# Small tables of the opening moved between engines, and a fourth output buffer

## The chip, the cores and the metric

The kernel runs on one core of one Trainium2 chip. Times are device microseconds of one execution. The core has a matrix engine (TensorE, PE in the profile; its weight loads are PEld), VectorE (DVE), ScalarE (ACT), GpSimd (POOL) and SyncE (SP). Each runs its own queue of instructions in order, and the queues meet only at semaphores. DMAs are issued from SP, ACT or POOL.

## The reference

```python
def _attn_ref(x):                      # x: 8 x 3072 x 256
    X = np.fft.fft(x, axis=1)
    X = np.fft.fft(X, axis=2)
    return X.real.astype(np.float32)

def _moe_ref(x, mu_k, mu_r, w_k, w_v, w_r):
    x_prev = np.concatenate([np.zeros((B, 1, D)), x[:, :-1, :]], axis=1)
    xk = mu_k * x + (1.0 - mu_k) * x_prev
    xr = mu_r * x + (1.0 - mu_r) * x_prev
    k = np.maximum(xk @ w_k, 0.0)      # w_k: 256 x 1024
    v = k * k @ w_v                    # w_v: 1024 x 256
    r = 1.0 / (1.0 + np.exp(-(xr @ w_r)))
    return r * v
```

The output of the first function is the `x` of the second: the real part of a two-dimensional Fourier transform over sequence and features, then a mixing of neighbouring positions and a gated layer.

## The kernel before, in words

The transform is made of matrix products. The 3072 positions are split as 48 times 64. Because only the real part is wanted, a position is first added to its mirror image (`fold`, on DVE, from the plain rows `xp` and the mirrored rows `xm`; the mirrored rows come by indirect DMA on POOL, `load_m` and `load_m0`). Then come three products: over the 48 with the table `w_pm` (`a_sum` in batch 0, lines L582), over the features with `w_eo` (`d_units`, L604), and over the 64 with the twiddled table `m_cs` (`c_sums`, L646). Each product goes to PSUM and is evacuated to SBUF as fp16 by ACT or DVE. After that `diff` and `mix` make the mixed inputs, and chunks of 512 positions go through `k_piece` (L757), `r_item` (L784) and `v_tile` or `v_part` (L798, L810). ACT takes the rectifier and the sigmoid, DVE the squares and, in `v_out` (L820), the gate `r` times `v` into an output tile `o`, which SP writes to memory (L828). There are 48 chunks. A table of steps says what other work stands between the matrix products of the chunks, so that the transform of the next batches runs beside the layer of the present one.

Nothing of the tables is loaded; all are computed in the opening. POOL makes ramps and indices by `iota`. From them DVE makes small rows in `rw_0`, `rw_1` and `rw_turn`, the latter holding two rows, TO and SG, used for a permutation `turn`. PE multiplies pairs of rows into phases (`outer`, L334), DVE or ACT scales these to angles in whole numbers (`u_w` for `w_pm`, `ueo` for `w_eo`, `ang` for `m_cs`; `m_angles` on DVE for the first six columns, `m_angles_2` on ACT for the rest) and wraps them by a bitwise and (`wrap_angles`), and ACT takes the sine (L386 and L388, `eo_sine` L486, `m_sine` L440). The helper `ts` on L265 is DVE's tensor_scalar, so that line stands for many small operations. After the sines ACT loads the table of the sigmoid (L839) and begins to evacuate the first products (L521).

The mixing weights mu come as two rows, `mu_row`, by two DMAs from ACT's queue. `mu_rows(a)` copies them in the wanted order into `mu_p` with three copies for each half (L226, on ACT in the kernel before). PE turns `mu_p` into columns with four tiny matrix products into `mu_ps` (L843), to which two `outer` products of the rows TO and SG are added; DVE copies the six columns to `muf_t` (L851).

PE also runs matmuls with zeros (`keep_busy`, L206, the fillers), whose results nobody reads. Four of them are the first thing PE does, eight stand behind the products of the angles, and four between the mu products and the first `a_sum`.

The order of every engine's instructions is the order in which the program writes them: at the end `pin_order` ties each instruction to the one before it on its engine. So an instruction that waits holds up all that is written behind it for the same engine. In the opening the program writes, in this order: the loads and index rows; the small rows and their products; the angles; then

```python
    m_angles_2(ang_ps[1], NJ1, NJ)
    ts(w_pm[:, 0:2, WA:WA + WB], w_pm[:, 0:2, WA:WA + WB], math.sqrt(0.5), MUL)
    ts(w_pm[:, 2], w_pm[:, 0], -1.0, MUL)
    wrap_angles(NJ1, NJ)
    m_sine(0, NJ1)
    eo_sine()
    m_sine(NJ1, NJ)
```

then the first fold, the mu products, the four zero matmuls, `a_sum(0, 0, 0)`, the next fold and so on, and after `a_sum(0, 0, 4)` the function `loads()`, which on POOL makes the index rows `row_i` (L434), gathers the two halves of `wk`, patches `w_eo` (L508, L509), clears two columns of `m_cs` (L447) and loads `wv_sb` (L455).

Of the kernel before, what the change touches and what calls it, by code (L numbers as in the profile page):

```python
# [13 lines left out]
AF = mybir.ActivationFunctionType  # L14
# [6 lines left out]
def _v(ap, extra_offset, free_dims):  # L21
    new_ap = [list(ap.ap[0])] + [[s, c] for (s, c) in free_dims]
    return dataclasses.replace(ap, offset=ap.offset + extra_offset, ap=new_ap)
# [16 lines left out]
def kernel(  # L40
# [10 lines left out]
    nc = tc.nc  # L51
# [3 lines left out]
    P = 128  # L55
# [3 lines left out]
    NJ, NJ1 = 14, 6  # L59
# [4 lines left out]
    y_pool = ctx.enter_context(tc.tile_pool(name="y_sb", bufs=1))  # L64
    mix_pool = ctx.enter_context(tc.tile_pool(name="mix", bufs=1))
    k2_pool = ctx.enter_context(tc.tile_pool(name="k2", bufs=2))
    o_pool = ctx.enter_context(tc.tile_pool(name="o", bufs=3))
    psum = ctx.enter_context(tc.tile_pool(name="psum", bufs=1, space=bass.MemoryType.PSUM))


# [10 lines left out]
    def ps_v():  # L81
        return ps_slot("V", 2, 512)
# [23 lines left out]
    V = nc.vector  # L106
# [32 lines left out]
    def gather(dst, src, idx):  # L139
        nc.gpsimd.indirect_dma_start(dst, None, src, bass.IndirectOffsetOnAxis(ap=idx, axis=0))  # L140

    def load_m(b, h, o, n, idx):
        gather(xm_t[b, h][0:parts(b), XM0 + o:XM0 + o + 256 * n],
               x.rearrange("b (s r) d -> (b s) (r d)", r=n), idx)

    def load_m0(b):
        if b == 0:
            gather(xm_00[:, 1:257], x.rearrange("b s d -> (b s) d"), idx_0[:, 0:1])
        else:
            load_m(b, 0, 2048, 1, (idx_g0 if b > 1 else idx_0)[:, b:b + 1])  # L150
# [52 lines left out]
    def keep_busy(n, ps, cols=512):  # L203

        for _ in range(n):
            nc.tensor.matmul(out=ps[:, 0:cols], lhsT=zeros,  # L206
                             rhs=_v(zeros, 0, [(0, cols // P), (1, P)]), start=True, stop=True)
# [9 lines left out]
    mu_row = const.tile([2, 256], FP32)  # L217
    mu_p = const.tile([2, 2, P], FP32)
# [4 lines left out]
    def mu_rows(a):  # L223
        for p0, f0, step, n in (((0, 0, 1, 1), (1, 2, 2, 63), (64, 1, 2, 64)),
                                ((0, 128, 1, 1), (1, 254, -2, 63), (64, 255, -2, 64)))[a]:
            nc.scalar.activation(out=mu_p[:, a, p0:p0 + n], in_=_v(mu_row, f0, [(step, n)]),  # L226
                                 func=AF.Copy)

    for h in range(2):
        x_tiles(0, h)  # L230
# [19 lines left out]
    load_m(0, 1, 0, 4, idx_4[:, 1:2])  # L250
    iota(idx_0, pattern=[[S, B]], base=S, channel_multiplier=-32)
    iota(idx_0[0:1], pattern=[[S, B]], base=0, channel_multiplier=0)
    load_m0(0)

    g_all = const.tile([P, NU // 2, 256], FP16)

# [6 lines left out]
    def ts(out, in0, s1, op0, s2=None, op1=None):  # L263
        kw = {} if op1 is None else {"op1": op1}
        V.tensor_scalar(out=out, in0=in0, scalar1=s1, scalar2=s2, op0=op0, **kw)  # L265

    MUL, ADD = ALU.mult, ALU.add
# [9 lines left out]
    TO, SG = range(2)  # L277
# [5 lines left out]
    def rv(n, o, *dims, k=1):  # L283
        return _v(rw_0[0:k], P * n + o, list(dims)) if n < 6 else _v(rw_1, P * (n - 6) + o, list(dims))

    def tv(n, o, *dims):
        return _v(rw_turn, P * n + o, list(dims))

    one = ramp[0:1]
    C_0, C_1 = [(64, 2), (1, 32)], [(64, 2), (1, 32)]  # L290
# [7 lines left out]
    V.memset(rv(PH0, 64 + 47, (1, 1)), -S / 4)  # L298
    V.memset(rv(PHS0, 64 + 15, (1, 1)), S / 4)
    V.memset(rv(ONE, 0, (1, 1)), 1.0)  # L300

# [8 lines left out]
    for i in range(2):  # L312
        nc.scalar.activation(out=unit[:, i:i + 1], in_=g_i[0:2], func=AF.Copy, bias=1.0 - i,
                             scale=2.0 * i - 1.0)
    mu_rows(0)
    mu_rows(1)

    ts(rv(JR, 0, (1, P)), one, 0.0, ADD)
    ts(rv(PN, 0, (2, 64), (1, 2)), _v(one, 0, [(2, 64), (0, 2)]), 0.0, ADD)
# [49 lines left out]
    ts(ph_c, prep[:, P_C:P_C + 4], float(TURN) / S, MUL)  # L369


    V.memset(tv(SG, 0, (1, P)), 1.0)
    V.memset(tv(SG, 32, *C_1), -1.0)
    V.memset(tv(SG, 47, (64, 2)), 1.0)
    for c in range(2):
        ts(tv(TO, 32 * c, (64, 2), (1, 32)), _v(one, 32 * c, [(64, 2), (1, 32)]),
           32.0 - 64.0 * c, ADD)
    ts(tv(TO, 15, (32, 4)), _v(one, 15, [(32, 4)]), 0.0, ADD)

    ang_ps = [ps_v(), ps_v()]  # L380
    m_outer(ang_ps[0], 0, NJ1)
# [2 lines left out]
    for g in range(2):  # L384
        kw = dict(func=AF.Sin, bias=sc[:, 2 + g:3 + g], scale=sc[:, g:g + 1])
        nc.scalar.activation(out=_v(w_pm, g, [(WA + WB, 2), (2, 2), (4, NU)]),  # L386
                             in_=_v(u_w, 0, [(0, 2), (NU, 2), (1, NU)]), **kw)
        nc.scalar.activation(out=_v(w_pm, WA + g, [(WA + WB, 2), (2, NU)]),  # L388
                             in_=_v(u_w, 2 * NU, [(0, 2), (1, NU)]), **kw)

    def wrap_angles(j0, j1):
        ts(ang[:, :, j0:j1], ang[:, :, j0:j1], TURN - 1, ALU.bitwise_and)

    def m_angles_2(ps, j0, j1):
        for c in range(2):
            nc.scalar.activation(out=ang[:, c, j0:j1], in_=ps[:, 0:64 * (j1 - j0)],
                                 func=AF.Identity, bias=ph_c[:, 2 * c:2 * c + 1],
                                 scale=float(TURN) / S)

    def m_angles(ps, j0, j1, z=0):  # L400
        for c in range(2):
            for k0, k1, n in ((j0, j0 + z, 2 * c + 1), (j0 + z, j1, 2 * c))[1 - z:]:
                ts(ang[:, c, k0:k1], ps[:, 64 * (k0 - j0):64 * (k1 - j0)], float(TURN) / S, MUL,
                   ph_c[:, n:n + 1], ADD)
        if j0 == 0:
            wrap_angles(j0, j1)

    m_angles(ang_ps[0], 0, NJ1, 1)
    for c in range(2):
        ts(ueo[:, :, c], _v(prep, P_E, [(64, 2), (1, 64)]), TURN / 256.0, MUL,  # L410
           0.75 * (1 - c) * TURN, ADD)
    ts(ueo, ueo, TURN - 1, ALU.bitwise_and)
    keep_busy(NF[0], fill)

    turn = const.tile([P, P], FP16)
# [23 lines left out]
    def m_sine(j0, j1):  # L439
        nc.scalar.activation(out=m_cs[:, 0:2, j0:j1], in_=ang[:, :, j0:j1], func=AF.Sin,  # L440
                             bias=m_pi, scale=TWO_PI / TURN)
# [43 lines left out]
    def eo_sine():  # L485
        nc.scalar.activation(out=w_eo.rearrange("p a b -> p (a b)"),  # L486
                             in_=ueo.rearrange("p a c b -> p (a c b)"), func=AF.Sin,
                             bias=m_pi, scale=TWO_PI / TURN)
# [325 lines left out]
    def v_out(c, tb, n):  # L814
        b, m, i = c
        o = o_pool.tile([P, 2, 256], FP32, name="o" if n == 2 else f"o{tb}",
                        bufs=3 if n == 2 else 1)
        t0 = tb + 1 - n

        V.scalar_tensor_tensor(out=o.rearrange("p a b -> p (a b)")[:, 0:256 * n],  # L820
                               in0=st["v", t0][:, 0:256 * n], scalar=16.0,
                               in1=st["r", c][:, 256 * t0:256 * (t0 + n)],
                               op0=ALU.mult, op1=ALU.mult)
        for s in range(2):
            k = 24 * m + 8 * i + 2 * t0 + s
            dst = dataclasses.replace(out[b, k:k + 1, :], ap=[[48 * D, 64], [2 * D, n], [1, D]])
            eng = nc.scalar if s and c == chunks[-1] else nc.sync
            eng.dma_start(out=dst, in_=o[64 * s:64 * s + 64, 0:n])  # L828

    m_angles_2(ang_ps[1], NJ1, NJ)
    ts(w_pm[:, 0:2, WA:WA + WB], w_pm[:, 0:2, WA:WA + WB], math.sqrt(0.5), MUL)
    ts(w_pm[:, 2], w_pm[:, 0], -1.0, MUL)
    wrap_angles(NJ1, NJ)
    m_sine(0, NJ1)
    eo_sine()
    m_sine(NJ1, NJ)
    nc.scalar.activation(out=warm, in_=zeros[:, 0:1], func=AF.Sigmoid)  # L839
    fold(0, 0, 1, 4)  # L840
# [44 lines left out]
    for a in range(2):  # L885
        t = x_t["t", a] = mix_pool.tile([P, 24, 64], FP16, name=f"t{a}")
        nc.scalar.activation(out=t[:, 0:4],
                             in_=_v(first, 64 * a, [(128, 2), (512, 2), (1, 64)]), func=AF.Copy,
# [140 lines left out]
    for b in range(B):  # L1029
# [9 lines left out]
        if t < B:  # L1039
# [6 lines left out]
            c = [(c_pairs, t, 8 * n, (8, 8, 8, 4)[n], EV[n]) for n in range(4)]  # L1046
# [21 lines left out]
    for step in range(nk + LAG):  # L1068
        if step < nk:
            k_piece(chunks[step // 4], step % 4)  # L1070
        due(step, "x")
        v = v_steps.get(step)
        if v and step not in early_v:
            v_tile(*v)
        if step in p_steps:
            v_part(*p_steps[step])
        due(step, "e")
        if step + 1 in early_v:
            v_tile(*v_steps[step + 1])
        early = step in OUT_FIRST  # L1080
        for v in o_steps.get(step, ()) if early else ():
            v_out(*v)
        due(step, "w")
        for v in () if early else o_steps.get(step, ()):
            v_out(*v)
        if step < 4 * EARLY + 4:
            square(chunks[step // 4], step % 4, 1, step in SQUARE_A)
        elif step < nk and step % 2:
            square(chunks[step // 4], step % 4)
# [32 lines left out]
```

## Time and profile before

| | us |
|---|---|
| median of 3 runs (431.78 to 432.16) | 432.0 |
| the profiled execution | 432.3 |
| its span, first to last instruction | 430.5 |
| PE busy in it | 422.7 (98%) |
| DVE busy | 360.8 (84%) |
| ACT busy | 320.3 (74%) |
| POOL busy | 62.7 (15%) |

In the rows shown below, a row of the timeline reads: start, duration, engine, line of the kernel, operation, what it writes and reads by the program's names, shapes, and how many instructions are merged; in brackets stands how long the engine was idle before and what ended that. A row of the chain gives start, duration and what the end of the run hung on then. A row of the stretches gives the stretch, its length, the busy time of PE, PEld, DVE, ACT and POOL with their counts, the granted share of PE's clock, the share of the DMA engines and GB/s. A row of the waits gives who waited, for whom, the total, how often and the longest. Matmuls are pipelined, so the end of one lies beyond the start of the next.

### The profile page before, as it was taken

To read this page: it belongs to the slowest core of one execution; us is meant where nothing else is said; L and a number is where in the kernel's file an instruction comes from. 1 tells how busy PE (TensorE), PEld (TensorE's weight loads), DVE (VectorE), ACT (ScalarE), POOL (GpSimd) and SP (SyncE) were. 2 spreads that over 40 slices of the span, in tenths; PEclk is the share of its full clock that TensorE was granted. 3 is DMA by queue.
4 is the path that set the end of the run, shared out by engine and by line. 5 is a ranking of instruction groups with operands and counts; after the bars stand their busy time and mean duration, and the time that the engine had idled before them with its cause. 6 is when DMAs were issued, how large, how long until landed. Compare 5 with 4: busy or idle time off the path is not lost.

```text
span 430.5 us, 9306 instructions
## 1 busy us (share of the span) xinstructions
PE 422.7 (98%) x3858; PEld 298.3 (69%) x3858; DVE 360.8 (84%) x547; ACT 320.3 (74%) x373; POOL 62.7 (15%) x96
## 2 busy tenths in 40 slices
PE   7999999999999999999999999999999999999996
PEld 3666766777777776776677777777776767766765
DVE  8898989997998879988898988989799847997453
ACT  7888898867778778776877777777786867666661
POOL 7686202000050001400041000500000000000000
PEclk9999999999999999999999999999999999999999
DMA  8999926323286232933259223763232322223233
GB/s 172 143 146 197 224 58 123 81 50 73 61 144 153 59 77 56 191 95 75 52 113 188 64 50 74 136 158 75 50 75 49 75 69 55 68 64 72 67 73 99
DMA packets 35102, 42.06 MB, mean 98 GB/s; under 512 B 4114, under 2 KB 31092, under 8 KB 35060
## 3 DMA queue, kind: packets, MB, share of 16 engines
q1 hardware_dynamic: 27488, 25.41, 23.6%
q0 software_dynamic: 7264, 15.80, 22.4%
q8 instruction: 30, 0.49, 0.5%
q10 hardware_dynamic: 308, 0.26, 0.2%
q14 instruction: 12, 0.10, 0.1%
HBM read 32.08 MB, written 25.17 MB: 133 GB/s over the span
## 4 chain that ended last, share of the span: by engine, by line
PE 89%; DVE 4%; DMA 3%; ACT 3%; issue 0%; ACTq 0%; SPq 0%; DVEq 0%
PE psV L798 36%; PE psW L757 36%; PE psW L784 9%; PE psW L604 2%; DMA out_dram<-o 2%; PE psW L678 1%; PE psW L564 1%; PE psV L810 1%; DVE k L777 1%; DMA mu_row<-in_moe_mu_r_dram 1%; ACT a L521 1%; DVE o L820 1%; PE psW L646 0%; DVE x L722 0%; DVE d L699 0%; ACT m_cs L440 0%
## 5 line engine op out<-in xcount | busy, mean ns | idle before, releaser
L767 ACT ACTIVATE rl<-psW 128x1024 f16<-128x1024 f32 x192 | 195.4, 1025 | 93.2 <-PE psW L757 89.5
L757 PE MATMUL psW<-x,wk 128*128 128x512 f16 (+1 forms) x776 | 195.6, 377 | 0.5
L798 PE MATMUL psV<-wv_sb,k 128*128 128x256 f16 x1424 | 184.1, 273 | 0.0
L798 PEld LDWEIGHTS <-k 128*128 128x128 f16 x1424 | 137.0, 98 | 35.7
L777 DVE TENSOR_TENSOR k<-rl 128x2048 f16<-128x2048 f16 (+1 forms) x101 | 116.2, 1151 | 33.5 <-ACT rl L767 33.0
L757 PEld LDWEIGHTS <-wk 128*128 128x128 f16 x776 | 74.8, 98 | 53.5 <-issue 1.3
L820 DVE SCALAR_TENSOR_TENSOR o<-psV,r 128x512 f32<-128x512 f32 (+1 forms) x97 | 65.8, 681 | 15.9 <-PE psV L798 13.5
L722 DVE TENSOR_TENSOR x<-y,t 128x1536 f16<-128x1536 f16 (+2 forms) x72 | 61.6, 861 | 2.1
L784 PE MATMUL psW<-wr,x 128*128 128x256 f16 x384 | 49.8, 273 | 0.0
L789 ACT ACTIVATE r<-psW 128x1024 f16<-128x1024 f32 x48 | 48.9, 1018 | 0.8 <-PE psW L784 0.8
L784 PEld LDWEIGHTS <-x 128*128 128x128 f16 x384 | 37.5, 98 | 14.3 <-issue 0.2
L463 POOL IOTA gate<- 1x1 int32 x6 | 2.1, 356 | 199.2 <-DVE gate L462 199.2
L521 ACT ACTIVATE a<-psW 128x832 f16<-128x832 f32 x31 | 25.9, 862 | 1.4 <-PE psW L564 1.4
L521 ACT ACTIVATE g_all<-psW 128x1024 f16<-128x1024 f32 (+5 forms) x37 | 25.6, 694 | 0.4 <-PE psW L627 0.2
L140 POOL DMA_INDIRECT xm<-in_x_dram,idx_g x18 | 23.5, 1304 | 5.5 <-issue 5.2
L171 DVE TENSOR_TENSOR p<-xp,xm 112x2304 f16<-112x2304 f16 (+6 forms) x19 | 21.6, 1139 | 0.0
L711 DVE TENSOR_SCALAR t<-d,muf_t 128x1536 f16<-128x1536 f16 (+2 forms) x40 | 20.8, 529 | 0.0
L711 DVE TENSOR_SCALAR t<-d,mu_m 128x1536 f16<-128x1536 f16 x32 | 19.7, 615 | 0.0
L604 PEld LDWEIGHTS <-a 128*128 128x128 f16 x208 | 14.0, 98 | 6.5 <-ACT a L521 0.6
L182 DVE TENSOR_TENSOR eo<-p 112x1152 f16<-112x1152 f16 (+3 forms) x28 | 17.9, 678 | 0.0
L521 ACT ACTIVATE pq<-psW 128x1024 f16<-128x1024 f32 (+1 forms) x18 | 15.2, 880 | 2.3 <-PE psW L678 2.3
L699 DVE TENSOR_TENSOR d<-y 128x1664 f16<-128x1664 f16 (+5 forms) x19 | 16.7, 878 | 0.0
(137 smaller groups left out, 217.5 us busy)
## 6 DMA issues: line engine op xcount, KB each, us to landing
out_dram<-o SPq DMA_DIRECT2D x189, 128.0 KB, 2.4
xp<-in_x_dram POOLq DMA_DIRECT2D x12, 216.0 KB, 4.4
xp<-in_x_dram POOLq DMA_DIRECT2D x13, 192.0 KB, 7.7
xp<-in_x_dram POOLq DMA_DIRECT2D x2, 384.0 KB, 6.8
wv_sb<-in_moe_w_v_dram POOLq DMA_DIRECT2D x1, 512.0 KB, 7.3
xp<-in_x_dram SPq DMA_DIRECT2D x1, 480.0 KB, 4.1
xp<-in_x_dram POOLq DMA_DIRECT2D x1, 432.0 KB, 5.5
xm<-in_x_dram,idx_g POOLq DMA_INDIRECT x18, 8.4
```

Of the source, the lines that this page charges most:

```text
L140: nc.gpsimd.indirect_dma_start(dst, None, src, bass.IndirectOffsetOnAxis(ap=idx, axis=0))
L521: nc.scalar.activation(out=out_ap, in_=in_ap, func=AF.Copy)
L604: nc.tensor.matmul(out=ps[:, o:o + 128], lhsT=a_t[b][:, e, 2 * (u0 + i):2 * (u0 + i) + 2, :], rhs=w_eo[:, e], start=True, stop=True)
L711: V.tensor_scalar(out=dst, in0=src, scalar1=mu, scalar2=None, op0=ALU.mult)
L722: V.tensor_tensor(out=_v(x_t[b, j, m], o, [(64 * step, hi - lo), (step, 64)]), in0=y_t[b][:, lo + 3 * m:hi + 3 * m, a], in1=x_t["t", a][:, ...
L757: nc.tensor.matmul(out=st["k", ds][:, 512 * hs + lo:512 * hs + hi], lhsT=wk_sb[m][a][:, 128 * fc:128 * fc + 128], rhs=xk[:, a, 512 * i + l ...
L767: nc.scalar.activation(out=st["rl"][:, 2 * ds:2 * ds + 2], in_=st["k", ds].rearrange("p (f t) -> p f t", f=2), func=AF.Relu, bias=0.0, sca ...
L777: V.tensor_tensor(out=k2_t[c][:, lo:hi], in0=r, in1=r, op=ALU.mult)
L784: nc.tensor.matmul(out=ps[:, 256 * tb:256 * tb + 256], lhsT=x_t[b, 1, m][:, a, 512 * i + 128 * tb: 512 * i + 128 * tb + 128], rhs=wr_sb[m] ...
L789: nc.scalar.activation(out=st["r", c], in_=ps, func=AF.Sigmoid)
L798: nc.tensor.matmul(out=st["v", tb - h][:, 256 * h:256 * h + 256], lhsT=k2_t[c][:, fc, 128 * tb:128 * tb + 128], rhs=wv_sb[:, fc], start=(f ...
L820: V.scalar_tensor_tensor(out=o.rearrange("p a b -> p (a b)")[:, 0:256 * n], in0=st["v", t0][:, 0:256 * n], scalar=16.0, in1=st["r", c][:, ...
```

## The change

Six things are edited.

1. The six copies of `mu_rows` go from ACT to POOL, and their place goes from behind the `unit` rows to behind the angles. `load_m0(0)`, the gather of the first mirrored rows, is written at that place too, ahead of the copies.
2. The three memsets of the row SG stay on DVE and are written earlier, ahead of `g_i`.
3. The three operations that make the row TO go from DVE to ACT.
4. The angles `ueo` of the feature table are made ahead of the first `m_angles`, and their sine, `eo_sine`, ahead of both `m_sine`.
5. `wrap_angles(NJ1, NJ)` is written ahead of the two scalings of `w_pm`.
6. The pool of output tiles `o` has four buffers in place of three.

```diff
-    o_pool = ctx.enter_context(tc.tile_pool(name="o", bufs=3))
+    o_pool = ctx.enter_context(tc.tile_pool(name="o", bufs=4))
@@ mu_rows
-            nc.scalar.activation(out=mu_p[:, a, p0:p0 + n], in_=_v(mu_row, f0, [(step, n)]),
-                                 func=AF.Copy)
+            nc.gpsimd.tensor_copy(out=mu_p[:, a, p0:p0 + n], in_=_v(mu_row, f0, [(step, n)]))
@@ behind the index rows
-    load_m0(0)
@@ behind the memset of ONE
+    V.memset(tv(SG, 0, (1, P)), 1.0)
+    V.memset(tv(SG, 32, *C_1), -1.0)
+    V.memset(tv(SG, 47, (64, 2)), 1.0)
@@ behind the unit rows
-    mu_rows(0)
-    mu_rows(1)
@@ behind ph_c
-    V.memset(tv(SG, 0, (1, P)), 1.0)
-    V.memset(tv(SG, 32, *C_1), -1.0)
-    V.memset(tv(SG, 47, (64, 2)), 1.0)
     for c in range(2):
-        ts(tv(TO, 32 * c, (64, 2), (1, 32)), _v(one, 32 * c, [(64, 2), (1, 32)]),
-           32.0 - 64.0 * c, ADD)
-    ts(tv(TO, 15, (32, 4)), _v(one, 15, [(32, 4)]), 0.0, ADD)
+        nc.scalar.activation(out=tv(TO, 32 * c, (64, 2), (1, 32)),
+                             in_=_v(one, 32 * c, [(64, 2), (1, 32)]), func=AF.Copy,
+                             bias=32.0 - 64.0 * c)
+    nc.scalar.activation(out=tv(TO, 15, (32, 4)), in_=_v(one, 15, [(32, 4)]), func=AF.Copy)
@@ angles
-    m_angles(ang_ps[0], 0, NJ1, 1)
     for c in range(2):
         ts(ueo[:, :, c], _v(prep, P_E, [(64, 2), (1, 64)]), TURN / 256.0, MUL,
            0.75 * (1 - c) * TURN, ADD)
     ts(ueo, ueo, TURN - 1, ALU.bitwise_and)
+    m_angles(ang_ps[0], 0, NJ1, 1)
     keep_busy(NF[0], fill)
@@ v_out
-                        bufs=3 if n == 2 else 1)
+                        bufs=4 if n == 2 else 1)
@@ ahead of the first fold
     m_angles_2(ang_ps[1], NJ1, NJ)
+    wrap_angles(NJ1, NJ)
+    load_m0(0)
+    mu_rows(0)
+    mu_rows(1)
     ts(w_pm[:, 0:2, WA:WA + WB], w_pm[:, 0:2, WA:WA + WB], math.sqrt(0.5), MUL)
     ts(w_pm[:, 2], w_pm[:, 0], -1.0, MUL)
-    wrap_angles(NJ1, NJ)
+    eo_sine()
     m_sine(0, NJ1)
-    eo_sine()
     m_sine(NJ1, NJ)
```

## The prediction

> **What bounds the kernel now.** I read the page first, then the busy time by stretches, then the chain in order of time and the timeline of the opening.
>
> ```profile
> span 430.5 us, 9306 instructions
> PE 422.7 (98%) x3858; PEld 298.3 (69%) x3858; DVE 360.8 (84%) x547; ACT 320.3 (74%) x373; POOL 62.7 (15%) x96
> ```
> ```profile
> 20.00:25.00 5.00, 4.87 (x34) 2.86 (x34) 4.96 (x14) 5.00 (x8) 4.20 (x9) 1.00 1.05 178
> 40.00:45.00 5.00, 4.43 (x39) 3.47 (x37) 3.72 (x7) 3.57 (x5) 0.29 (x2) 1.00 1.04 184
> ```
> ```profile
> 25.00:40.00 15.00, 15.00 (x122) 10.28 (x121) 14.55 (x35) 12.99 (x16) 12.79 (x15) 1.00 0.96 169
> 50.00:60.00 10.00, 9.88 (x106) 6.72 (x105) 9.10 (x13) 9.03 (x12) 0.00 (x0) 1.00 0.52 123
> 60.00:420.00 360.00, 360.00 (x3316) 255.57 (x3314) 302.68 (x388) 267.83 (x290) 28.39 (x36) 1.00 0.40 87
> ```
>
> The second figure of a stretch is its length, the next PE's busy time. From 60 to 420 PE never pauses; between 20 and 60 it lacks 0.13, 0.57 and 0.12 us. So the change can gain after 20 us at most these 0.82 us, and all else is decided by how early or late the dense part starts. What starts it is a chain through the opening:
>
> ```profile
> 1.31 3.26 DMA mu_row<-in_moe_mu_r_dram
> 5.07 0.48 ACT mu_p L226 x3
> ...
> 10.35 1.28 ACT L839
> 11.85 2.71 ACT a L521 x4
> 14.60 0.40 PE psV L604 x4
> ```
>
> ACT waits for the mu rows, copies them, makes the sines, loads a table, and evacuates the first products `a`; at 14.60 PE starts on them (`d_units`). That point is my mark. Beside ACT, PE and DVE are nearly as late:
>
> ```profile
> 7.41 0.60 PE L843 MATMUL psV<-unit,mu_p 2*128 2x2 f32 x4
> ...
> 8.00 1.04 PE L206 MATMUL psW<-zeros 128*128 128x512 f16 x4
> 10.29 1.70 PE L582 MATMUL psW<-w_pm,p 96*128 96x208 f16 x16 [1.25 <-DVE p L173]
> 12.82 1.07 PE L582 MATMUL psV<-w_pm,p 96*128 96x208 f16 x10
> 8.81 1.21 DVE L171 TENSOR_TENSOR p<-xp,xm 96x1024 f16<-96x1024 f32 x1
> 10.14 0.70 DVE L171 TENSOR_TENSOR p<-xp,xm 96x1024 f16<-96x1024 f16 x1
> ...
> 13.99 0.56 ACT L521 ACTIVATE a<-psV 128x416 f16<-128x416 f32 x1
> ```
>
> PE's last `a` product ends at 13.89 and the last evacuation starts at 13.99. A gain on ACT alone is worth 0.1 us. And PE's order is fixed: the mu products (L843) and four fillers stand ahead of the first `a_sum` at 10.29.
>
> **The change part by part.**
>
> Copies of mu leave ACT, with their wait:
>
> ```profile
> 3.34 0.28 ACT L313 ACTIVATE unit<-g_i 2x1 f32<-2x1 int32 x2
> 4.67 0.89 ACT L226 ACTIVATE mu_p<-mu_row 2x1 f32<-2x1 f32 x6 [1.05 <-DMA mu_row<-in_moe_mu_r_dram]
> 5.46 0.61 ACT L386 ACTIVATE w_pm<-u_w,sc 128x104 f16<-128x104 int32 x1
> 3.54 2.22 PE L334 MATMUL psV<-rw 128*128 128x384 f16 x6
> 4.06 0.20 DVE L265 TENSOR_SCALAR u_w<-u_w 128x78 int32<-128x78 int32 x1
> 4.29 0.17 DVE L372 MEMSET rw_turn<- 1x128 f16 x1
> 5.12 1.37 DVE L265 TENSOR_SCALAR rl<-psV,ph_c 128x64 int32<-128x64 f32 x4
> 6.53 0.71 DVE L265 TENSOR_SCALAR rl<-rl 128x768 int32<-128x768 int32 x1
> ```
>
> The sines need `u_w`, ready at 4.26. The three SG memsets and the turn's rows fill DVE's time from 4.29 to 5.12; the memsets, moved ahead, fall partly into idle time there and delay what follows by some 0.15, an estimate from half their place, so the sines start near 4.45, not 5.46. The turn's three rows on ACT, at 0.14 each as two of the `unit` row, end near 4.0, inside the wait that was there; without that wait they would cost 0.4. `m_angles_2` then waits for PE's angles, 5.76 plus 0.15. So ACT is ahead by some 0.85 rather than 1.0, and its table load ends near 10.8.
>
> On DVE the rows go (0.83 less 0.15 and a few waits) and `ueo` passes ahead of the angles, so their wrap ends near 7.3, about where it ended (7.24); `eo_sine` ahead of `m_sine` covers ACT until then, so that exchange costs nothing. DVE reaches the first fold near 8.3 instead of 8.81. So far the gain is real, but PE must take it up.
>
> The copies now stand on POOL, behind `load_m0`. POOL's order of the rest is unchanged: nothing of POOL stood between the old and the new place of that gather.
>
> ```profile
> 7.34 0.12 POOL L252 IOTA idx<- 1x8 uint32 x1
> 8.05 0.95 POOL L140 DMA_INDIRECT xm<-in_x_dram,idx  x1 [0.59 <-POOL idx L252]
> 9.01 0.69 POOL L434 IOTA row_i<- 64x2 uint32 x4
> 12.56 0.24 POOL L508 TENSOR_SCALAR w_eo<-g_i 128x1 f16<-128x1 int32 x1
> 12.71 0.47 POOL L509 TENSOR_SCALAR w_eo<-g_i 128x1 f16<-128x1 int32 x1
> 14.98 0.55 POOL L493 TENSOR_SCALAR order<-order_i 128x128 f16<-128x128 int32 x1
> 12.68 0.41 DVE L171 TENSOR_TENSOR p<-xp,xm 96x256 f16<-96x256 f32 x1
> ```
> So the copies start at 9.0, where the index rows start now. That is the heart of it: mu_p was there at 5.56, and now comes no sooner than 9.0 plus six copies. PE stands at L843 until then, and behind it in PE's queue are the four fillers and every `a_sum`.
>
> A POOL copy of this form is not in the trace. From below, six at 0.12 (L252) give 0.7, at the index rows' pace of 0.17 1.0. From above, six at 0.55 (L493, 128 wide) give 3.3. The nearest are L508 and L509, small reads and writes of the same form, 0.24 and 0.47: six take 1.4 to 2.8. I take 2.0, as the longer of the two ran while DVE's fold of 12.68 did, and ended 0.09 after it; the copies meet the folds of 8.3 to 10.5 in the same way. Call T the time at which mu_p is ready: T = 11.0, bounds 9.7 and 12.3.
>
> [...]
>
> From T to the mark: L843's start to the end of the fillers is 9.04 − 7.41 = 1.63, less 0.17 of the last one's drain, which the next matmul overlaps: 1.46. From the first `a_sum` to the mark is 14.60 − 10.29 = 4.31, of which some 0.17 was one more wait for a fold, at 11.1: 4.14. New mark = T + 5.6 = 16.6, against 14.60: 2.0 us late; break-even is T = 9.0, the very time at which the copies begin. DVE (`muf_t` waits for L843, then three folds, done near 14.1) and ACT (free at 10.9) are both ahead of PE's new times.
>
> POOL's later work shifts by the same 2.0: index rows, wk, eo_rest, wv. wk's first use, wv's first use and `eo_rest` follow the mark, which shifts as much, so this costs nothing; were POOL alone late, wk would come first.
>
> The fourth buffer:
>
> ```profile
> 39.06 0.69 DVE L820 SCALAR_TENSOR_TENSOR o<-psV,r 128x512 f32<-128x512 f32 x1
> 41.24 0.69 DVE L820 SCALAR_TENSOR_TENSOR o<-psV,r 128x512 f32<-128x512 f32 x1 [1.48 <-DMA out_dram<-o]
> ```
> ```profile
> PE psV L810 <- DVE o L820: 0.6, 1, 0.6
> ```
> The fourth output waits 1.48 for the first one's transfer, and PE 0.6 for DVE. With a fourth buffer it starts at 39.8; PE's wait goes. The transfer stays as slow, but the fifth output then needs the first buffer, which this same wait shows free at 41.2. Gain 0.57, the whole gap of that stretch; at least 0, and at most 0.7 with part of the 0.12.
>
> Sum: +2.0 − 0.6 = +1.4. The profiled execution took 432.3 (span 430.5 and 1.8 around it): 433.7. The median of the runs, 432.0, is 0.3 lower; I leave the sum on the profiled one.
>
> **The rivals.**
>
> *The clock falls* (slower still). PE now idles from 7.4, where L843 starts before, plus the 0.15, to T: 3.4 us instead of 1.25.
>
> ```profile
> 426.40:428.60 2.20, 0.00 (x0) 0.00 (x0) 0.42 (x1) 0.00 (x0) 0.00 (x0) 1.00 0.82 228
> 428.60:430.50 1.90, 0.00 (x0) 0.00 (x0) 0.00 (x0) 0.00 (x0) 0.00 (x0) 0.52 0.04 12
> 0.99 1.89 PE L206 MATMUL psW<-zeros 128*128 128x512 f16 x4 [0.99 <-DVE xm L234]
> ```
> At the end of the kernel the granted clock fell to half 2.2 us after the last matmul, and four cold fillers took 1.89 where four warm ones take 1.04. If it falls in the opening, the products from T on run at half speed until it returns. Somewhere between the cold fillers, over at 2.88, and the warm ones of 8.00 it returned the first time; taking 2 to 4 us at half speed, 1 to 2 us are lost, 1.5 in the middle: 432.3 + 1.4 + 1.5 = 435.2. Against it: 1.25 idle did not trigger it, and the fall at the end may have had its own reason. It decides from an idle time somewhere above 1.25.
>
> [...]
>
> *The copies are cheap* (same). At the index rows' pace, with no hold by the folds, T = 10.0: mark 1.0 late, buffer 0.57 back, +0.4: 432.7. It holds up to T = 10.4. For it speaks the pace of POOL's small work; against it L509.
>
> *Faster*. If `load_m0` starts at once behind its iota, without the 0.59, at 7.5, the gather ends at 8.4, and with copies at half of L252's 0.12 T is 8.8: PE stops being last, and the folds, 0.5 earlier, set the mark: −0.5 − 0.6, 431.2. It decides from T = 8.7, where mark and buffer together give 0.9; every term has to fall the good way.
>
> *The buffer brings nothing*, since DVE's early output only moves PE's wait to another: 434.3; the stretch shows no other wait of PE, so this lies inside the range.
>
> **How the numbers follow.** Warm clock with T from 10.5 to 12.3, 433.2 to 435.0 (435.6 if the buffer fails): 0.43. Clock falls, 434.3 to 436.7: 0.32. Cheap copies, 432.4 to 433.2: 0.19. Faster, near 431.2: 0.06. The predicted time is the first one's 433.7. The range 432.2 to 436.1 leaves out the faster case, the low edge of the cheap one and the top of the clock's. A change of 0.2% is 0.9 us, about what a measurement can tell here: slower 0.75, same 0.19, faster 0.06.
>
> **What would show it.** Right: L843 stands at about 11.0 with a wait for POOL's mu_p, the first `a_sum` near 12.5, `d_units` near 16.6, ACT idle before its `a` evacuations, and no wait of DVE's fourth output for a transfer. Fillers behind L843 taking 1.9 instead of 1.04 would show the clock. L843 before 9.5 would prove me wrong in the price of the copies; a mark before 14.6, in the claim that PE's queue stands behind them.

## The result, and the profile after

The kernel after the change takes 435.23 us in the median (435.11 to 436.7), the one before on the same chip 432.16 (431.78 to 433.63): a ratio of 1.007, 95% interval 1.0044 to 1.0097. The change makes the kernel slower. The forecast was slower, at 433.7; the measured median is that of the rival *the clock falls*, 435.2.

The profiled execution after took 436.7, with a span of 434.9. Its page and its stretches, in the same columns as before (stretch, length, PE, PEld, DVE, ACT, POOL, clock, DMA share, GB/s):

```profile
span 434.9 us, 9302 instructions
PE 426.6 (98%) x3858; PEld 300.7 (69%) x3858; DVE 360.6 (83%) x544; ACT 320.6 (74%) x370; POOL 65.5 (15%) x102
```
```profile
20.00:25.00 5.00, 4.67 (x71) 3.51 (x69) 4.29 (x16) 3.69 (x10) 2.05 (x4) 1.00 0.66 83
25.00:40.00 15.00, 14.79 (x119) 9.64 (x118) 14.84 (x40) 13.02 (x18) 12.34 (x19) 1.00 0.93 160
40.00:45.00 5.00, 5.00 (x37) 3.43 (x36) 4.91 (x10) 4.97 (x6) 4.39 (x5) 1.00 1.07 203
60.00:420.00 360.00, 360.00 (x3341) 255.80 (x3340) 304.03 (x390) 269.62 (x294) 28.39 (x36) 1.00 0.40 86
```

From 60 to 420 PE still never pauses. The 0.57 us that PE lacked from 40 to 45 are gone. So the loss was made in the opening, and TensorE's timeline shows it:

```profile
6.07 2.71 PE L206 MATMUL psW<-zeros 128*128 128x512 f16 x8
10.77 1.08 PE L843 MATMUL psV<-unit,mu_p 2*128 2x2 f32 x4 [1.99 <-POOL mu_p L226]
...
11.83 1.89 PE L206 MATMUL psW<-zeros 128*128 128x512 f16 x4
13.51 2.98 PE L579 MATMUL psW<-w_pm,p 96*128 96x208 f16 x16
...
19.74 0.40 PE L601 MATMUL psV<-w_eo,a 128*128 128x128 f16 x4
```

The mark, the first `d_units` (L604 before, L601 here), went from 14.60 to 19.74, 5.14 late. PE waits 1.99 for POOL's `mu_p`. Then the four fillers take 1.89 where they took 1.04, and the first sixteen `a_sum` products 2.98 where they took 1.70: half speed. The wait delays the mark once, the half clock a second time.

To see which time ran at half clock, I cut the opening into stretches of 3.41 us. In the trace of the kernel after, the clock records begin at 7.71 and change at 11.12, 17.95 and 434.37, that is after 1, 2 and 122 times 3.413 us; in that of before they begin at 5.42 and change once, 124 times 3.413 later. So both lie on such a grid, each with a phase of its own. First the kernel after, then the one before, each on its own grid:

```profile
7.71:11.12 3.41, 1.42 (x7) 0.59 (x5) 3.02 (x7) 3.39 (x4) 3.06 (x7) 1.00 1.06 197
11.12:14.53 3.41, 3.29 (x15) 2.04 (x15) 2.19 (x7) 0.22 (x2) 2.73 (x9) 0.50 0.20 20
14.53:17.95 3.42, 3.42 (x21) 2.74 (x19) 0.00 (x0) 1.73 (x2) 2.63 (x7) 0.50 0.94 142
```
```profile
5.42:8.83 3.41, 3.41 (x20) 1.61 (x18) 3.31 (x11) 3.41 (x9) 2.45 (x5) 1.00 1.01 200
8.83:12.25 3.42, 2.17 (x21) 1.67 (x21) 3.32 (x9) 3.39 (x6) 2.73 (x9) 1.00 0.90 149
```

After the change, a stretch in which PE was busy 1.42 of 3.41 us (42%) is followed by two at half clock. In the execution shown of before, the stretch that holds its 1.25 us gap was busy 2.17 of 3.42 (63%), and the clock stayed whole.

The other engines are as the prediction had them, but for one wait. Rows of the kernel after:

```profile
4.55 0.62 ACT L383 ACTIVATE w_pm<-u_w,sc 128x104 f16<-128x104 int32 x1 [0.39 <-DVE u_w L263]
...
15.14 0.86 ACT L518 ACTIVATE a<-psW 128x832 f16<-128x832 f32 x1 [3.79 <-PE psW L579]
```
```profile
7.62 0.69 DVE L263 TENSOR_SCALAR rl<-rl 128x1024 int32<-128x1024 int32 x1 [0.38 <-ACT rl L393]
...
8.56 1.21 DVE L171 TENSOR_TENSOR p<-xp,xm 96x1024 f16<-96x1024 f32 x1
```

ACT's sines start 0.91 earlier, at 4.55 instead of 5.46, and all of that is then spent idle: it waits 3.79 for PE's first `a`. DVE reaches the first fold at 8.56 rather than 8.81.

### The profile page after: what moved, and what is told of

Its sections match the earlier page's. It is cut to its first block, busy times and chain, and to the rows that moved or that the text cites. A ratio compares the mean times of both kernels' runs of the same rounds, so it can differ in the third digit from the quotient of the medians.

```text
span 434.9 us, 9302 instructions
## 1 busy us (share of the span) xinstructions
PE 426.6 (98%) x3858; PEld 300.7 (69%) x3858; DVE 360.6 (83%) x544; ACT 320.6 (74%) x370; POOL 65.5 (15%) x102
## 4 chain that ended last, share of the span: by engine, by line
PE 95%; POOL 2%; DVE 1%; issue 0%; ACT 0%; POOLq 0%; ACTq 0%
PE psW L754 38%; PE psV L795 36%; PE psW L781 10%; PE psV L807 3%; PE psW L601 2%; PE psW L675 1%; PE psW L561 1%; PE psW L579 1%; POOL xm L140 1%; PE psW L643 1%; PE psW L206 1%; POOL mu_p L226 0%; DVE x L892 0%; ACT rl L764 0%; DVE x L735 0%
## 5 line engine op out<-in xcount | busy, mean ns | idle before, releaser
L140 POOL DMA_INDIRECT xm<-in_x_dram,idx_g x18 | 24.5, 1359 | 5.5 <-issue 5.5
L601 PEld LDWEIGHTS <-a 128*128 128x128 f16 x208 | 14.0, 98 | 6.5 <-ACT a L518 0.5
## 6 DMA issues: line engine op xcount, KB each, us to landing
xp<-in_x_dram POOLq DMA_DIRECT2D x1, 432.0 KB, 4.9
```

The costliest lines, as they stand in the source:

```text
L601: nc.tensor.matmul(out=ps[:, o:o + 128], lhsT=a_t[b][:, e, 2 * (u0 + i):2 * (u0 + i) + 2, :], rhs=w_eo[:, e], start=True, stop=True)
```

## The experiments

Each ratio is to the kernel before on the same chip. An execution is said to keep the clock when its mean granted clock is above 0.996, and to lose it otherwise; one stretch of 3.41 us at half lowers the mean over 432 us by 0.004. The mean shows only falls: ahead of a trace's first clock record (5.42 in the kernel before) the views print 1.00, although four fillers take 1.89 there (at 0.99), as at a granted 0.50 after the change, against 1.04 later. So a rise that comes late does not lower the mean.

### The kernel after again

The kernel is unchanged; the question is whether every execution loses the clock.

> The changed kernel as it is, beside the kernel before on the same chip, for more executions. Theory W: every execution holds one or two stretches of 3.4 us at half clock in the opening, so the times lie in two groups, near 435.2 and 436.6, and none comes near the 433.9 that it takes with the clock kept whole by more zero matmuls. Rival: some executions keep the clock and lie near 433.8.

435.33 (433.65 to 437.39) against 432.53: 1.0052 (1.003 to 1.0075). With the first measurement there are 17 executions, and they fall into three groups:

| executions of the kernel after | mean clock | time, us |
|---|---|---|
| 4 keep it | 0.998 to 1.0 | 433.65 to 434.21 |
| 9 lose some | 0.994 to 0.995 | 435.11 to 435.81 |
| 4 lose more | 0.991 to 0.992 | 436.54 to 437.39 |

So there are executions near 433.9, and my theory that there would be none is wrong. The profile of this run is one of the middle group. Timeline, then two stretches on its own grid:

```profile
10.78 0.88 PE L843 MATMUL psV<-unit,mu_p 2*128 2x2 f32 x4 [1.33 <-POOL mu_p L226]
```
```profile
9.05:12.46 3.41, 1.96 (x12) 1.04 (x11) 2.44 (x6) 2.28 (x3) 3.03 (x14) 1.00 0.71 124
12.46:15.88 3.42, 3.42 (x19) 2.70 (x18) 1.47 (x6) 1.18 (x2) 2.88 (x6) 0.50 0.56 85
```

With the same POOL times, the grid lies elsewhere, and the eight fillers ahead of L843 took 3.37 us instead of 2.71, so that the gap is 1.33: the poorest stretch is busy 1.96 (57%), and one stretch at half clock follows, not two. One costs some 435.3 − 433.75 = 1.6 us (433.75 is the median of the four that kept the clock).

### Fillers that cover the wait

The kernel after, with 19 fillers in place of 8 ahead of the mu products, so that PE has no gap while it waits for POOL:

```diff
-    NF = (8, 4, 1, 3, 0, 3, 0)
+    NF = (19, 4, 1, 3, 0, 3, 0)
```

> The changed kernel with 19 in place of 8 zero matmuls behind the products of the angles: eleven more at 0.216, so that PE works until about 10 to 11 while it would wait for mu_p; all else as changed. Theory W, clock part: the clock stays whole, the four fillers behind L843 take 1.04 and d_units stands at T + 5.6, 16.8: the time is that of the warm case, 433.4 to 433.8. Rival N (the fall of the clock costs little, and the wait makes the whole 3.1): 435.

433.86 (433.54 to 434.25) against 432.04: 1.0032 (1.0016 to 1.0049), just above what I expected. All twelve executions kept the clock.

```profile
6.07 5.73 PE L206 MATMUL psW<-zeros 128*128 128x512 f16 x19
11.73 0.60 PE L843 MATMUL psV<-unit,mu_p 2*128 2x2 f32 x4
...
17.25 0.40 PE L601 MATMUL psV<-w_eo,a 128*128 128x128 f16 x4
```

Work that nobody reads makes the kernel after 1.4 us faster by the medians (0.9 to 1.6 by the ratios), though the fillers run to 11.80, past the time at which `mu_p` is ready (11.22), so that L843 starts at 11.73, not at 10.77 as after the change. So the clock is one part of the loss, and the later mark alone, 17.25 here, the other.

### The copies on GpSimd alone

The kernel before, with only the copies moved, behind the gather `load_m0`:

```diff
-            nc.scalar.activation(out=mu_p[:, a, p0:p0 + n], in_=_v(mu_row, f0, [(step, n)]),
-                                 func=AF.Copy)
+            nc.gpsimd.tensor_copy(out=mu_p[:, a, p0:p0 + n], in_=_v(mu_row, f0, [(step, n)]))
@@ behind load_m0(0)
+    mu_rows(0)
+    mu_rows(1)
```

> The kernel before, with one edit: the six copies of mu stand on POOL behind load_m0. Theory W (PE's queue waits for mu_p, and the clock falls in that wait): L843 starts near 11, d_units near 18 to 20, and since the fourth buffer is missing the time is 0.5 above the changed kernel's 435.2: 435.7. Rival O (the other edits of the opening or the later wk and wv do it): below 433.0. If the clock stays warm in this kernel, 434.2.

436.54 (435.33 to 438.6) against 432.04: 1.0092 (1.0061 to 1.0122), and every execution lost the clock. Its wait of PE, and POOL's row:

```profile
PE psV L842 <- POOL mu_p L226: 4.0, 1, 4.0
```
```profile
9.00 2.46 POOL L226 COPY mu_p<-mu_row 2x1 f32<-2x1 f32 x6
```

This edit alone makes the whole loss. By the medians it is 1.2 to 1.3 us slower than the whole change and 0.8 above what I expected, though the intervals of the ratios overlap; it lacks the fourth buffer, and in its profile PE is idle for 4.0 us.

### All but the copies

The kernel after, with the copies on ACT where they were:

```diff
-            nc.gpsimd.tensor_copy(out=mu_p[:, a, p0:p0 + n], in_=_v(mu_row, f0, [(step, n)]))
+            nc.scalar.activation(out=mu_p[:, a, p0:p0 + n], in_=_v(mu_row, f0, [(step, n)]),
+                                 func=AF.Copy)
@@ behind the unit rows
+    mu_rows(0)
+    mu_rows(1)
@@ behind load_m0(0)
-    mu_rows(0)
-    mu_rows(1)
```

> The changed kernel, with the six copies of mu back on ACT behind the unit rows; all else as changed. Theory W: no wait of PE at L843, no fall of the clock, the opening within 0.2 of the kernel before since ACT is last again, and the buffer's 0.57 gained: 431.5. Rival O: it stays above 433.5.

432.35 (431.96 to 432.52) against 432.04: 0.9998 (0.9985 to 1.0011). The loss is gone, all executions keep the clock, and the gain I expected does not come.

```profile
5.97 0.61 ACT L386 ACTIVATE w_pm<-u_w,sc 128x104 f16<-128x104 int32 x1
```
```profile
8.61 0.86 DVE L264 TENSOR_SCALAR rl<-rl 128x1024 int32<-128x1024 int32 x1 [1.36 <-ACT rl L396]
9.71 1.21 DVE L171 TENSOR_TENSOR p<-xp,xm 96x1024 f16<-96x1024 f32 x1
```
```profile
15.38 0.40 PE L604 MATMUL psV<-w_eo,a 128*128 128x128 f16 x4
```

The turn's rows now stand in ACT's queue behind the copies, which wait for the mu rows. So the sines come 0.5 later than before, at 5.97; ACT's angles follow them, DVE waits 1.36 for those, and because the wrap was written ahead of the scalings of `w_pm`, the first fold, at 9.71, waits with it. The mark is 0.78 later than before. Rows on ACT are free only if ACT's wait for mu stands behind them or is gone.

### The fourth buffer alone

```diff
-    o_pool = ctx.enter_context(tc.tile_pool(name="o", bufs=3))
+    o_pool = ctx.enter_context(tc.tile_pool(name="o", bufs=4))
@@ v_out
-                        bufs=3 if n == 2 else 1)
+                        bufs=4 if n == 2 else 1)
```

> The kernel before with four output buffers and nothing else. Theory W: the one wait of an output for a transfer, 1.48, and PE's 0.57 behind it go: 431.6, and PE's gap between 40 and 45 us closes. Rival: PE's wait moves elsewhere and the time stays at 432.1.

431.82 (431.46 to 433.02) against 432.04: 0.9987 (0.9973 to 1.0002). Its stretch and its DVE row:

```profile
40.00:45.00 5.00, 5.00 (x43) 3.85 (x41) 4.97 (x9) 3.71 (x5) 1.56 (x3) 1.00 1.06 193
```
```profile
38.95 1.29 DVE L820 SCALAR_TENSOR_TENSOR o<-psV,r 128x512 f32<-128x512 f32 x2
```

The two outputs now follow each other, and PE's 0.57 are filled. The medians differ by 0.22, by 0.29 if only executions that kept the clock, 10 of its 12, are compared (431.605 against 431.895); the interval allows anything from −1.2 to +0.1. So the mechanism is shown and a worth of 0.57 neither confirmed nor excluded.

### Memsets in place of the copies

The kernel after, with six memsets of the same rows on POOL in place of the copies, so that nothing is read there (all mu are 0.5, the mixing weights are left out):

```diff
-            nc.gpsimd.tensor_copy(out=mu_p[:, a, p0:p0 + n], in_=_v(mu_row, f0, [(step, n)]))
+            nc.gpsimd.memset(mu_p[:, a, p0:p0 + n], 0.5)
```

> The changed kernel with six memsets of the same places of mu_p in place of the six copies, on POOL at the same place: nothing is read (the mixing then takes 0.5 for every mu, so that part of the computation is left out). Theory H (the copies of 0.72 and 0.77 were held by DVE's folds because they read SBUF; the free price is 0.2): memsets at 0.1 to 0.17 are not held, L843 starts at 9.9 to 10.1 in place of 11.2, PE's idle time falls by 1.2, and the time to 433.0 if the clock stays whole, 434.5 if it still falls. Rival P (a POOL instruction beside a fold is slow whatever it does): two of the six last over 0.5 and L843 stands near 11 again, 435.2.

432.06 (431.83 to 432.75) against 432.52: 0.998 (0.9966 to 0.9994). All executions keep the clock. That is 0.9 below what I expected: L843 starts at 9.40, right behind the fillers, and not at 9.9 to 10.1. First the copies of the kernel after, in the groups of POOL from 9 to 11.3 by shape (busy, mean ns), then three rows of the run with memsets:

```profile
L226 POOL COPY mu_p<-mu_row 2x64 f32<-2x64 f32 x2 | 1.0, 496 | 0.0
L226 POOL COPY mu_p<-mu_row 2x1 f32<-2x1 f32 x2 | 0.9, 462 | 0.0
L226 POOL COPY mu_p<-mu_row 2x63 f32<-2x63 f32 x2 | 0.5, 228 | 0.0
```
```profile
9.09 0.46 POOL L226 MEMSET mu_p<- 2x1 f32 x6
```
```profile
8.55 1.21 DVE L171 TENSOR_TENSOR p<-xp,xm 96x1024 f16<-96x1024 f32 x1
```
```profile
14.92 0.40 PE L601 MATMUL psV<-w_eo,a 128*128 128x128 f16 x4
```

One element per row costs 462 ns in the mean and 63 elements 228, so the length is not what counts. Of each pair with a high mean one copy is long: 0.72 for the first of all, which began at 9.09 inside the fold of 8.56 to 9.77, and 0.77 for the one that began at 9.95, with the fold of 9.94 to 10.62; each ends within 0.1 us of that fold's end. The other four take 0.20 to 0.23. The memsets, over at 9.55, lie wholly inside the same fold and are not held by it. The hold shows as the copy's own time and not as a wait at a semaphore ahead of it (idle time 0.0 in the rows): by these rows the two queues met outside the semaphores too. That agrees with theory H, but a memset differs from a copy in more than that it reads nothing, and what about the copies was held was not separated.

### The copies ahead of the gather

```diff
-    load_m0(0)
     mu_rows(0)
     mu_rows(1)
+    load_m0(0)
```

> The changed kernel with load_m0 and the copies of mu in the other order on POOL; nothing else. Theory W: the copies run from 7.5, L843 starts between 8.6 and 9.9 by how far DVE's wrap and fold hold them, load_m0 and its landing come 1 to 2 later and the last fold may wait for it; d_units at 14.4 to 15.3, the clock stays whole: 431.4 to 432.3, at least 2.9 under the changed kernel. Rival O (POOL's copies as such cost it, not their place): 434 or more.

433.35 (432.72 to 434.58) against 432.52: 1.0009 (0.9995 to 1.0022).

```profile
7.44 1.48 POOL L226 COPY mu_p<-mu_row 2x1 f32<-2x1 f32 x6
9.08 1.72 POOL L140 DMA_INDIRECT xm<-in_x_dram,idx  x1 [0.16 <-POOL mu_p L226]
```
```profile
15.15 0.38 PE L601 MATMUL psV<-w_eo,a 128*128 128x128 f16 x4
```

It is 1.9 below the kernel after in the median, yet above what I expected. `mu_p` is ready at 8.92 rather than 11.2, but the gather, 0.95 long before, takes 1.72 beside the folds and ends 1.8 later than before, and POOL's later work is late with it. The mark is 0.55 later than before, and not for POOL: in the profiled execution the eight fillers took 3.62 us, about twice the 1.89 of before, as at half speed, and L843 follows them:

```profile
6.07 3.62 PE L206 MATMUL psW<-zeros 128*128 128x512 f16 x8
9.62 0.60 PE L843 MATMUL psV<-unit,mu_p 2*128 2x2 f32 x4
```

Another 0.54 of PE is lost between 25 and 40, where the kernel before lost nothing:

```profile
25.00:40.00 15.00, 14.46 (x115) 9.20 (x115) 13.77 (x32) 12.20 (x15) 11.87 (x15) 1.00 1.08 196
```

Together that is 1.1, but PE's 0.57 from 40 to 45, which the kernel before lacks, is gained here. So some 0.5 is explained of the 1.2 by which its executions that kept the clock (433.32) exceed those of before (432.09), and the rest stays open.

### The copies on VectorE

The kernel after, with the copies on DVE behind the scalings of `w_pm`, and the wrap of the later angles behind them:

```diff
-            nc.gpsimd.tensor_copy(out=mu_p[:, a, p0:p0 + n], in_=_v(mu_row, f0, [(step, n)]))
+            V.tensor_copy(out=mu_p[:, a, p0:p0 + n], in_=_v(mu_row, f0, [(step, n)]))
@@ ahead of the first fold
-    wrap_angles(NJ1, NJ)
     load_m0(0)
-    mu_rows(0)
-    mu_rows(1)
     ts(w_pm[:, 0:2, WA:WA + WB], w_pm[:, 0:2, WA:WA + WB], math.sqrt(0.5), MUL)
     ts(w_pm[:, 2], w_pm[:, 0], -1.0, MUL)
+    mu_rows(0)
+    mu_rows(1)
+    wrap_angles(NJ1, NJ)
```

> The changed kernel with the copies of mu on DVE, behind the two scalings of w_pm, and the wrap of the later angles behind them, so that DVE has work while ACT makes those angles. Theory W: no engine waits for mu_p; the first fold starts at 8.5 to 8.8 as the copies take 0.5 to 0.9, ACT keeps its 0.85, d_units stands at 14.3 to 14.6, and with the buffer the time is 431.2 to 431.6, below both kernels. Rival: DVE's folds come later than before, 9.2 or more, and it ends at 432.

432.73 (432.11 to 433.33) against 432.52: 0.9991 (0.9977 to 1.0005). The gain expected is not there, nor is the rival's reason: the first fold starts at 8.63, as expected.

```profile
8.07 2.55 POOL L140 DMA_INDIRECT xm<-in_x_dram,idx  x1 [0.58 <-POOL idx L251]
```
```profile
14.94 0.38 PE L601 MATMUL psV<-w_eo,a 128*128 128x128 f16 x4 [0.65 <-POOL w_eo L506]
```

The same gather now takes 2.55 us. Wrap, first fold and second fold follow each other on DVE from 8.02 to 10.63, and the gather ends at 10.62, with the second fold, as the one of 1.72 above did (10.80). In the kernel before DVE had no gap either, yet the gather ended at 9.00, 0.2 into the first fold. POOL is then 1.6 late, PE waits 0.65 for POOL's last write to `w_eo`, and later 1.3 for a transfer that POOL issues behind that gather:

```profile
PE psW L754 <- DMA wk<-in_moe_w_k_dram,row_i: 1.3, 1, 1.3
```

So two long gathers end with the second fold, and the 0.95 of before ended inside the first; which of DVE's operations held the gather was not separated.

### The rows first on ScalarE

The run with all but the copies, mended by what it showed: the turn's rows stand ahead of the copies in ACT's queue, and the scalings ahead of the wrap in DVE's:

```diff
+    for c in range(2):
+        nc.scalar.activation(out=tv(TO, 32 * c, (64, 2), (1, 32)),
+                             in_=_v(one, 32 * c, [(64, 2), (1, 32)]), func=AF.Copy,
+                             bias=32.0 - 64.0 * c)
+    nc.scalar.activation(out=tv(TO, 15, (32, 4)), in_=_v(one, 15, [(32, 4)]), func=AF.Copy)
     mu_rows(0)
     mu_rows(1)
...
-    wrap_angles(NJ1, NJ)
     load_m0(0)
     ts(w_pm[:, 0:2, WA:WA + WB], w_pm[:, 0:2, WA:WA + WB], math.sqrt(0.5), MUL)
     ts(w_pm[:, 2], w_pm[:, 0], -1.0, MUL)
+    wrap_angles(NJ1, NJ)
```

> As the kernel with all of the change but the copies of mu (which stood on ACT as before, and ended 0.3 above the time expected), with two lines moved: the turn's rows on ACT ahead of the copies of mu, into ACT's wait for the mu rows, and the scalings of w_pm ahead of the wrap of the later angles, as before the change. Theory R (there the rows came behind the copies and pushed the sines from 5.46 to 5.97, and DVE, with the scalings and the first fold behind the wrap, waited for ACT's angles): the sines start at 5.45 to 5.55, the first fold at 8.7 to 8.9, d_units at 14.4 to 14.6; with the buffer 431.3 to 431.8. Rival: another part of the opening costs it and it stays at 432.3.

432.03 (431.34 to 432.61) against 432.53: 0.9975 (0.9955 to 0.9995). It is faster than both kernels, though 0.2 us above the range expected. An earlier mark is not the reason:

```profile
10.26 1.71 PE L582 MATMUL psW<-w_pm,p 96*128 96x208 f16 x16 [0.39 <-DVE p L173]
...
14.68 0.40 PE L604 MATMUL psV<-w_eo,a 128*128 128x128 f16 x4 [0.19 <-ACT a L521]
```

The mark, 14.68, is where it was. What differs is the clock: none of 12 executions lost it, against 8 of 23 of the kernel before on that chip. PE's gap ahead of `a_sum` is 0.39 here and 1.25 in the profile of before, but only part of that is the edit. The run with the fourth buffer alone has the opening of before, and its profile shows 0.58, because its eight fillers took 2.41 us instead of 1.89:

```profile
10.28 1.71 PE L582 MATMUL psW<-w_pm,p 96*128 96x208 f16 x16 [0.58 <-DVE p L173]
```

The kernel before's executions that kept it have a median of 432.22, so 0.3 of the gain of 0.5 goes with the clock and 0.2 is left, about what the buffer alone brought.

### The clock in the kernel before

That led to the kernel before itself. Beside these experiments 32 of its 110 executions lost the clock, at 433.0 to 435.6; those that kept it reach up to 433.4, but their medians in the four sets of runs are 431.9 to 432.2. Three runs touch its fillers. First, none behind the angles and none behind the mu products:

```diff
-    NF = (8, 4, 1, 3, 0, 3, 0)
+    NF = (0, 0, 1, 3, 0, 3, 0)
```

> The kernel before without the eight zero matmuls behind the angles and without the four behind L843: no work that counts is touched, but PE idles from about 5.5 to 7.5 and from 8 to 10.3. Theory C (idle PE alone, with no wait on the critical path, makes the clock fall): the products from 10.3 on run at half speed for one or two stretches of 3.4, and the time rises by 1.5 to 3 to 433.5 to 435. Rival: the fall needs the wait of the changed kernel or more than 3 us without a break; the time stays at 432.0.

434.05 (433.51 to 434.91) against 432.52: 1.0035 (1.002 to 1.005).

```profile
10.57 2.96 PE L582 MATMUL psW<-w_pm,p 96*128 96x208 f16 x16 [2.90 <-DVE p L173]
...
16.51 0.40 PE L604 MATMUL psV<-w_eo,a 128*128 128x128 f16 x4
```

`a_sum` starts 0.28 later than it did, at half speed, and the mark is 1.9 late. That costs 1.5 us in the median, 2.0 against the executions of before that kept the clock (432.09): the half clock with hardly any other change. The time is the one expected, but this profile does not show a fall:

```profile
6.64 0.98 PE L843 MATMUL psV<-unit,mu_p 2*128 2x2 f32 x4 [0.68 <-ACT w_pm L388]
```

Already here, ahead of the long gap, L843 takes 0.98 where it took 0.60, no stretch before the end reads less than 1.00, and the mean of this execution is 0.999. So in this execution, without the fillers, the clock had not yet risen. Seven of the twelve executions have a mean above 0.996 and take as long (433.51 to 434.91) as the five that lost it (433.90 to 434.30). The run gives the price of the half clock; it does not show that idle time alone makes the clock fall.

Second, nine fillers instead of four behind the mu products, to fill the gap of 1.25:

```diff
-    NF = (8, 4, 1, 3, 0, 3, 0)
+    NF = (8, 9, 1, 3, 0, 3, 0)
```

> The kernel before with nine instead of four filler matmuls behind the mu products, so that its 1.25 us of idle TensorE between the last filler (12.35) and the first a_sum matmul (13.60) is filled with five more at some 0.216 us each (8 in 1.73 us before), 1.1 us. Theory of the clock: the executions of the kernel before that lie 1.0 to 2.5 us above its others (27 of 87, with a mean clock of 0.996 or less) are those in which that gap cost a stretch of 3.41 us at half clock. Then here none of 12 has a clock of 0.996 or less, all lie between 431.4 and 432.4, and the median is 432.0, some 0.2 to 0.5 below the kernel before on the same chip. Rival: the clock of those executions falls for another reason; then 3 or 4 of 12 still lie above 433, and the median is the kernel before's.

432.23 (431.4 to 434.91) against 432.32: 0.9999 (0.9983 to 1.0015). One execution of 12 lost the clock, where I expected none; the kernel before lost it in 5 of 23 there. Third, the same with the fourth buffer:

```diff
-    NF = (8, 4, 1, 3, 0, 3, 0)
+    NF = (8, 9, 1, 3, 0, 3, 0)
...
-    o_pool = ctx.enter_context(tc.tile_pool(name="o", bufs=3))
+    o_pool = ctx.enter_context(tc.tile_pool(name="o", bufs=4))
@@ v_out
-                        bufs=3 if n == 2 else 1)
+                        bufs=4 if n == 2 else 1)
```

> The run before this one with a fourth output buffer as well. If the two gains add (0.57 for the buffer's wait, and the whole clock in every execution), the median is 431.4 (431.1 to 431.7), ratio near 0.997, and no execution has a clock of 0.996 or less; it would then do with two small edits as much as the version with the turn's rows first (432.03). Rival: the fillers delay a_sum by the queueing of a few matmuls when the folds come early, and 0.3 to 0.5 of it is lost, 431.8 to 432.0.

432.0 (431.6 to 432.59) against 432.32: 0.9991 (0.9979 to 1.0003), and no execution lost the clock. The gains did not add; the rival had it. The fillers are too long by a little:

```profile
8.76 2.12 PE L206 MATMUL psW<-zeros 128*128 128x512 f16 x9
10.71 1.59 PE L582 MATMUL psW<-w_pm,p 96*128 96x208 f16 x16
...
14.83 0.40 PE L604 MATMUL psV<-w_eo,a 128*128 128x128 f16 x4
```

These rows are from the run with three buffers. `a_sum` follows the ninth filler at 10.71, not the fold, 0.42 later than before, and the mark is 0.23 late. The two runs together lost the clock in 1 execution of 24, the kernel before in 5 of 23 beside them. Beside those 23 alone the lower share could be chance; against the 32 of all 110 that is unlikely. So the runs support that the gap causes the falls, and do not prove it; the one that remains, 434.91, is not explained.

## Why the prediction was right, and where wrong

**When mu is ready: right, and for the reason given.** T was put at 11.0 (9.7 to 12.3); it was 11.2. The copies were put at 2.0 us from 9.0:

```profile
8.06 1.03 POOL L140 DMA_INDIRECT xm<-in_x_dram,idx  x1 [0.59 <-POOL idx L251]
9.09 2.12 POOL L226 COPY mu_p<-mu_row 2x1 f32<-2x1 f32 x6
```

They took 2.12 from 9.09, held by two folds as the rows of L508 and L509 had suggested. Memsets, which the fold did not hold, took 0.46, and the loss was gone: the case *cheap copies* has its mechanism right and its condition unmet.

**From T to the mark: right for the warm clock.** The forecast was 5.6 us, a mark of 16.6. No profile shows an execution of the kernel after that kept the clock, but the run with 19 fillers shows that path at the whole clock: from L843 at 11.73 to the mark at 17.25 are 5.52. The sum let L843 start at T; after the change it started at 10.77, when the first half of `mu_p` was there. The four executions of the kernel after that kept the clock, 433.65 to 434.21, contain the 433.7 of the forecast, and against the kept ones of before on that chip they are 433.75 − 432.22 = 1.5 slower, where the sum said 1.4. That the two agree so closely is partly luck, because the buffer's 0.57 in the sum is not confirmed.

**ACT, DVE, rows and exchanges: right that they bring nothing.** ACT ahead by 0.85 was 0.91, and went into a wait of 3.79. DVE's first fold was put at 8.3 and came at 8.56: the step that had the wrap end near 7.3 missed that the wrap, now ahead of the scalings, waits 0.38 for ACT's angles. That the turn's rows are free on ACT held only because the wait for mu had left ACT; with it there they cost 0.5 (all but the copies).

**PE's idle time: too long.** The rival said 3.4 us; it was 1.99, since the eight fillers began at 6.07 rather than 5.59 and took 2.71 rather than 1.89, some of them still at half speed. In the second profile of the kernel after they took 3.37, and the idle time was 1.33.

**The buffer: right in the wait that goes,** unsettled in its worth, 0.57 against 0.2 to 0.3 measured between medians.

**The clock: the step that failed.** The sum's mechanism, a late mark at the whole clock, describes 4 of 17 executions; the median lies where the rival put it. The prediction held the warm clock the likeliest, 0.43 against 0.32, because "1.25 idle did not trigger it". That was read from one execution. 32 of 110 executions of the kernel before lost the clock in the same order of work, and 13 of 17 of the kernel after did, at 435.1 to 437.4, where the rival had 434.3 to 436.7. So the chances should have stood the other way round. The size of the term was right: 1.5 forecast, 1.6 measured between the groups of one and no lost stretch; that a second stretch can follow, some 3.1 in all, was not foreseen. The 2 to 4 us at half speed behind the 1.5 were an estimate that no row of before shows; the profiles show 3.42 in one execution of the kernel after and 6.83 in another. The forecast had the clock decide from an idle time "somewhere above 1.25". It fell after idle times of 1.33 and 1.99, in stretches of 3.41 us in which PE was still busy 57% and 42%, so a stretch without any matmul was not needed.

What stays open is whether the busy share of a stretch decides it. One at 63% did not lose it and one at 57% did, but the busy time counts L843's four 2x2 products, 0.88 to 1.08 us there, like any other matmul, and the second half-speed stretch of the kernel after follows one that reads 96% busy. No run varied that share alone. When the clock first rises was not varied alone either; it sets how long the fillers take (1.89 to 3.62 for the same eight), and so the gap behind them.

## What to carry over

An operation that TensorE's queue waits for is to be priced by when its new engine gets to it, not by how idle that engine is on average: here a move off an engine that had 0.1 us to gain made `mu_p` ready at 11.2 instead of 5.56. In this opening a wait of TensorE cost twice, once as delay and once through the clock: 19 fillers across the wait gave 1.4 us back, while five more across the shorter gap of the kernel before held `a_sum` and gained nothing in the median. An event that comes in some executions and not in others, here in 32 of 110, must be judged from the spread over many; that one profile lacks it says little.

## What the runs showed of the hardware that I had not expected

- The granted clock fell after gaps of PE of 1.33, 1.99 and 4.0 us in three profiles (to 0.50 in the stretches shown of the first two; 0.64 in the mean from 10 to 15 us in the third, the copies on GpSimd alone), for the kernel after in 13 of 17 executions; one stretch of 3.41 us at half cost about 1.6 us.
- When it first rises differs between executions: the same eight fillers took 1.89, 2.71 or 3.37 us, and without them the products still ran at half speed at 10.57 (2.96 us for sixteen, against 1.70).
- The kernel before pays this too, in 32 of 110 executions; the one version here that computes everything and beats it beyond its interval, the rows first on ScalarE, never lost the clock, and more than half of its gain goes with that.
- One indirect gather issued from POOL occupied it for 0.95, 1.72 or 2.55 us in runs that differ in what DVE did meanwhile.
- Six small copies on POOL cost 1.48 to 2.46 us, the shortest when they ended at 8.92, just after the first fold began, and six memsets of the same rows 0.46.
